# A small early read of w1's rows and a last tile cut 384 + 128, in a fused retention and MLP kernel

## The chip, the cores and the metric

The kernel runs on one core of a Trainium2 chip. The metric is device time in microseconds for one execution of the whole program. A core has five engines that run their own instruction streams in order: TensorE (PE, matrix multiplication), VectorE (DVE), ScalarE (ACT), GpSimd (POOL) and SyncE (SP, which here only issues transfers). Transfers between device memory and the core's own memory are issued from the queues of SP, ACT and POOL and carried out by 16 DMA engines.

## The reference

Two parts, one after the other. The first is a retention layer over 4 batches, 8 heads, 768 positions and a head size of 64; the second is a layer norm with a two-matrix MLP and a residual:

```python
for t in range(S):
    state = gamma * state + einsum('bhd,bhe->bhde', k[:, :, t], v[:, :, t])
    y[:, :, t] = scale * einsum('bhd,bhde->bhe', q[:, :, t], state)
x  = y.transpose(0, 2, 1, 3).reshape(B, S, 512)
xn = (x - mean(x)) / sqrt(var(x) + 1e-6) * g_ln
out = x + maximum(xn @ w_ch1, 0) @ w_ch2
```

`gamma` has one fixed value for each head. `w_ch1` is 512 x 2048, `w_ch2` is 2048 x 512; all inputs and the output are float32.

## The kernel before

**Tiles.** The 3072 positions are cut into 24 tiles of 128. The first four tiles are the first chunks of the four batches; after them come the five further chunks of each batch in turn. The recurrence is computed chunk by chunk: inside a chunk as a masked product of q and k (`pa`, L477), then with v (`py`, L505), between chunks through a state (`pd`, L551, with v scaled by GpSimd in `vg`, L539) that VectorE decays (`state`, L565) and TensorE multiplies with q (L501). VectorE takes the mean and variance (L520, L521) and subtracts the mean and multiplies by `g_ln` (`xn`, L515); ScalarE keeps a bf16 copy of the row (`x_all`, L526).

**The MLP.** The matrix w1 is loaded in four quarters of 512 columns and w2 in four quarters of 512 rows; each is converted to bf16 on the way, and such loads come from GpSimd's queue (L382; q, k and v on L374). Tiles are grouped by 1, 2 or 4. For each group TensorE multiplies the transposed `xn` with blocks of w1 (`mm`, L626; the block `ho` of 128 columns belongs to quarter `ho // 4`), ScalarE or, for the first tiles, VectorE applies the maximum with zero (L639, L641), and TensorE multiplies with w2 (`tp`, L664). VectorE scales by the reciprocal deviation and adds the residual (L673), and the result is stored (L680): from SP's queue, or from ACT's for a piece that doesn't begin at column 0. The last tile is done in two pieces of 256 columns, each with its 16 matmuls, its VectorE operation and its store.

**Transposes.** For the first eight tiles q, k (L437, L444) and `xn` (L579) are transposed by TensorE; from tile 8 on by DMA transposes from SP's queue (L459, L593).

**The order of the work.** Nothing is placed by hand. The kernel describes tasks with `plan.add` (engine, a cost in ns, a rank, what they come after, which buffer they take), and `Plan.order` plays a small model of the engines forward and emits each engine's instructions in the order that it finds: of all tasks that can start, the one with the earliest start, and at equal starts the one with the lower rank. Two numbers stand for the DMA engines: `sw_free`, when the queue of GpSimd's loads is believed to be empty, and `hw_free` for transfers of SP and ACT. A load pushes `sw_free` on by its cost (875 or 1250 ns for a tile of q, k or v, 2550 for a quarter of a weight) and is believed to be usable some time after. A transfer with a cost `hw` that finds loads queued pushes them too:

```python
            if t["hw"]:
                begun = max(at + 600, hw_free)
                queued = max(0, sw_free - begun)
                hw_free = begun + t["hw"] + min(queued, 2 * t["hw"])
                if queued:
                    sw_free += t["hw"] * 2 // 3
```

A load is not planned to be issued earlier than 7000 ns ahead of `sw_free`. The early loads follow the order of the list `first`, with v of tile 0 the first of them. `Plan.fill` puts dummy matmuls (L691) into holes of TensorE's plan up to 14 us. SP's early tasks are two loads of halves of k and q of tile 0 (L345) and the load of `g_ln` into `grow` (L312), in this order of rank; the first two have no `hw` cost in the plan and neither has `grow`. SP's next task after these is the first DMA transpose.

Of the kernel before, what the change touches and what calls it, by code (L numbers as in the profile page):

```python
# [9 lines left out]
FP32 = mybir.dt.float32  # L10
# [4 lines left out]
PE, ACT, DVE, POOL, SP = range(5)  # L15

CFG = {
    "T0": 8, "TX": 8, "groups": [1] * 8 + [2] * 4 + [4] * 2,
    "first": ["iota", "pos", "v0", "k1", "q1", "v1", "w1_0", "k2", "q2", "w1_1", "v2",
              "k3", "q3", "v3", "w1_2", "k4", "q4", "v4", "k5", "q5", "v5", "w1_3", "w2_0",  # L20
              "k6", "q6", "v6", "k7", "q7", "v7", "w2_1", "w2_2", "w2_3"],
    "bufs": {"qsb": 6, "ksb": 5, "vsb": 9, "qk": 8, "tr": 6, "vg": 3, "trq": 3, "trk": 3},
    "load_pad": 600, "w_pad": 1500, "lead": 32, "lead2": 32, "sq_at": 28000, "late_load": 1250, "step": 8, "pace": 8, "ahead": 3,
    "slack": 600, "tr_pad": 4000, "x_pad": 3000, "vg_pad": 1000, "fill": 0.8, "fill_end": 14000,
}

# [101 lines left out]
def kernel(  # L128
# [16 lines left out]
    nc = tc.nc  # L145

    B, H, S, D = q.shape
    DM = H * D
    DH = 4 * DM
    P = 128  # L150
    C = S // P
    NT = B * C
    KO = DM // P
# [31 lines left out]
    const = ctx.enter_context(tc.tile_pool(name="const", bufs=1))  # L185
# [12 lines left out]
    def take(pool, key, shape, dtype):  # L198
        held[pool, key] = pools[pool].tile(shape, dtype, name=pool, tag=pool)
        return held[pool, key]  # L200
# [5 lines left out]
    w1_v = moe_w_ch1.rearrange("(ko p) n -> p ko n", p=P)  # L206
# [21 lines left out]
    gb = const.tile([P, DM], FP32, name="gb")  # L228
    bns = const.tile([P, NT, 6], FP32, name="bns")
    mv = const.tile([P, NT, 2], FP32, name="mv")  # L230
    rstd = const.tile([P, NT], FP32, name="rstd")
    w1 = const.tile([P, KO, DH], BF16, name="w1")
    w2 = const.tile([P, HO, DM], BF16, name="w2")
# [55 lines left out]
    a = plan.add  # L289
# [18 lines left out]
    def c_gb(eng):  # L308
# [4 lines left out]
        out=grow, in_=moe_g_ln.rearrange("(o n) -> o n", o=1)), lat=2500)  # L313
# [85 lines left out]
        load(x, j, pool_rank.get(f"{x}_{j}" if x[0] == "w" else f"{x}{j}", 20 * i))  # L399
    for t, x in ((iota, "iota"), (ipos, "pos")):  # L400
        t["rank"] = pool_rank[x]

    unit, u, behind = {}, 0, []
    for g in range(NG):
# [12 lines left out]
    for t in range(NT):  # L417
        g, i = group_of[t]
# [6 lines left out]
    for t in range(NT):  # L425
# [31 lines left out]
        else:  # L457
            def e_tr(eng, t=t):
# [4 lines left out]
                   hw=1600, lat=TR_PAD)  # L463
# [67 lines left out]
        if c > 0:  # L531
            for cc in ([0, 1] if c == 1 else [c]):
                if cc == C - 1:
                    continue
                j = number[b, cc]
# [113 lines left out]

    loaded_w2 = [loaded["w2", i] for i in range(4)]  # L650
    for t, cols in [(t, slice(0, DM)) for t in range(NT - 1)] + [
            (NT - 1, slice(i * DM // 2, (i + 1) * DM // 2)) for i in range(2)]:
        g, i4 = group_of[t]
        hb, h0 = buf_of[g]
        key = ("tp", ("2", t, cols.start))
        w = cols.stop - cols.start
        dep = [relu[g, ho] for ho in range(0, HO, GMAX // GROUPS[g])]
        prev = None
        for part in range(4):
            def e_m2(eng, hb=hb, i=h0 + i4, key=key, part=part, cols=cols, w=w):  # L660
                if part == 0:
                    take(*key, [P, w], FP32)
                for ho in range(4 * part, 4 * part + 4):
                    nc.tensor.matmul(held[key], lhsT=held["h1", hb][:, ho, i * P:(i + 1) * P],  # L664
                                     rhs=w2[:, ho, cols], start=(ho == 0), stop=(ho == HO - 1))
            prev = a(PE, 865 * w // DM, 500 + unit["2", t] + part + (4 if cols.start else 0), e_m2,
                     dep[part * len(dep) // 4:(part + 1) * len(dep) // 4] + (loaded_w2 if part == 0 else [])
                     + ([prev] if prev else []),
                     key if part == 0 else None,
                     [("h1", hb)] + ([key] if part else []))  # L670

        def e_add(eng, t=t, key=key, cols=cols, w=w):
            nc.vector.scalar_tensor_tensor(  # L673
                out=take("osb", key, [P, w], FP32), in0=held[key], scalar=rstd[:, t:t + 1],
                in1=x_all[:, t, cols], op0=ALU.mult, op1=ALU.add)
        add = a(DVE, 750 * w // DM, -10, e_add, [prev, held["rs", t]], ("osb", key), [key])

        def e_st(eng, t=t, key=key, cols=cols):
            b, c = TILES[t]
            (nc.scalar if eng == ACT else nc.sync).dma_start(out=out_v[b, c, :, cols],  # L680
                                                             in_=held["osb", key])
        a(ACT if cols.start else SP, 400, 100, e_st, [add], uses=[("osb", key)], hw=450)
# [44 lines left out]
```

## Time and profile before

| | |
|---|---|
| median of 6 runs | 217.69 us (217.35 to 220.28) |
| profiled execution | 217.04 us |
| its span, first to last instruction | 215.0 us |
| mean granted TensorE clock | 0.998 |
| TensorE busy | 205.3 us (96%) |
| VectorE, ScalarE, GpSimd busy | 119.6, 83.8, 96.8 us |
| first use of w1 by TensorE | 13.0 us |
| last of GpSimd's quarters of weights issued | 34.3 us |

Times in the profile are microseconds from the start of the span unless marked ns. A line of a timeline gives the start, the length, the engine, the line of the program, the operation, `output<-input`, shapes and count, and in brackets the idle time before it and what ended that. "POOLq", "SPq" and "ACTq" are the queues' issuing instructions. The chain of waits follows the last instruction back to what released it, and so on to the start. A matmul's length is modelled, and runs of matmuls overlap by a fraction, so a busy TensorE isn't TensorE at its peak.

### The profile page before, as it was taken

What the parts mean: (1) busy time and instruction counts of PE and PEld (TensorE: products, weight loads), DVE (VectorE), ACT (ScalarE), POOL (GpSimd) and SP (SyncE); (2) the same over time, 40 slices, a digit from 0 to 9 for tenths busy, and PEclk for the clock granted to TensorE, in tenths of its full rate; (3) what the DMA queues carried; (4) which work ended last, traced back from release to release, by engine and by line L of the source; (5) the groups of instructions that cost most, each with busy time, mean ns of one, the idle gap of its engine ahead of it and who ended that gap; (6) DMA issues with size and microseconds to landing.
All of it is one profiled execution on the core that took longest, in us unless ns stands there. A gap on an engine that the chain in (4) does not pass through costs nothing.

```text
span 215.0 us, 4747 instructions
## 1 busy us (share of the span) xinstructions
PE 205.3 (96%) x1942; PEld 133.3 (62%) x1962; DVE 119.6 (56%) x230; ACT 83.8 (39%) x157; POOL 96.8 (45%) x151
## 2 busy tenths in 40 slices
PE   7968989999999999999999999999999999999993
PEld 3447979998755468677577667655454444444452
DVE  6767586992167775657997637866553411011121
ACT  5356675765420117245135324305554214442000
POOL 8998858735877745848776757000000000000000
PEclk9999999999999999999999999999999999999999
DMA  9999999999999999999999999921202121010212
GB/s 134 163 180 181 166 194 170 208 114 143 119 178 175 176 191 144 153 138 179 141 165 169 142 210 184 152 73 27 73 0 73 37 88 39 10 49 3 98 49 98
DMA packets 108359, 26.78 MB, mean 125 GB/s; under 512 B 101041, under 2 KB 105393, under 8 KB 108338
## 3 DMA queue, kind: packets, MB, share of 16 engines
q0 software_dynamic: 77024, 13.37, 84.8%
q1 hardware_dynamic: 30114, 12.72, 27.6%
q10 hardware_dynamic: 1200, 0.39, 0.7%
q8 instruction: 15, 0.25, 0.5%
q14 instruction: 6, 0.05, 0.1%
HBM read 27.27 MB, written 6.29 MB: 156 GB/s over the span
## 4 chain that ended last, share of the span: by engine, by line
PE 83%; POOL 10%; DMA 5%; issue 1%; DVE 0%; POOLq 0%
PE tp L664 38%; PE mm L626 35%; DMA w<-in_moe_w_ch_dram 5%; PE pa L477 3%; PE pd L551 2%; PE py L505 2%; POOL qsb L374 2%; PE py L501 2%; POOL v L374 2%; POOL w L382 1%; POOL k L374 1%; POOL vg L539 1%; POOL vsb L374 1%; POOL ksb L374 1%; POOL state L287 0%
## 5 line engine op out<-in xcount | busy, mean ns | idle before, releaser
L626 PE MATMUL mm<-xnt,w 128*128 128x128 bf16 (+2 forms) x896 | 93.4, 257 | 1.0 <-ACT xnt L203 1.0
L664 PE MATMUL tp<-w,h 128*128 128x512 bf16 (+1 forms) x381 | 86.9, 370 | 1.1 <-issue 0.2
L639 ACT ACTIVATE h<-mm 128x512 bf16<-128x512 f32 x91 | 54.4, 598 | 66.2 <-PE mm L626 65.8
L626 PEld LDWEIGHTS <-w 128*128 128x128 bf16 x896 | 66.2, 98 | 21.2 <-issue 1.0
L664 PEld LDWEIGHTS <-h 128*128 128x128 bf16 x400 | 37.7, 98 | 37.5
L673 DVE SCALAR_TENSOR_TENSOR osb<-tp,rstd,x_all 128x512 f32<-128x512 f32 (+1 forms) x25 | 18.2, 728 | 51.6 <-PE tp L664 51.5
L488 DVE TENSOR_TENSOR asb<-pa,mask 128x1024 bf16<-128x1024 f32 x24 | 29.3, 1221 | 12.9 <-PE pa L477 12.8
L520 DVE BATCH_NORM_STATS2 bns<-py 128x6 f32<-128x512 f32 x24 | 16.7, 694 | 17.0 <-PE py L505 17.0
L526 ACT CAST x_all<-py 128x512 bf16<-128x512 f32 x24 | 14.0, 584 | 28.6 <-DVE xn L515 28.0
L539 POOL TENSOR_TENSOR vg<-vsb,vsc 128x512 bf16<-128x512 bf16 x16 | 16.6, 1042 | 12.6 <-PE mm L626 5.5
L374 POOL DMA_DIRECT2D vsb<-in_v_dram x20 | 18.2, 909 | 0.8 <-issue 0.4
L515 DVE SCALAR_TENSOR_TENSOR xn<-py,mv,gb 128x512 bf16<-128x512 f32 x24 | 18.0, 751 | 0.9
L565 DVE TENSOR_TENSOR state<-pd,gch 64x256 bf16<-64x256 f32 x40 | 16.7, 418 | 2.5 <-PE pd L551 2.2
L374 POOL DMA_DIRECT2D qk<-in_q_dram x16 | 14.0, 877 | 2.7 <-issue 1.9
L374 POOL DMA_DIRECT2D qk<-in_k_dram x16 | 14.1, 883 | 1.4 <-issue 0.8
L387 POOL COPY scrap<-qk 1x1 bf16<-1x1 bf16 x30 | 5.3, 177 | 12.8 <-DMA qk<-in_q_dram 6.4
L466 DVE TENSOR_TENSOR trq<-tr,qsc 128x512 bf16<-128x512 bf16 x16 | 8.5, 530 | 2.9 <-DMA tr<-qk 2.8
L691 PE MATMUL pd<-zeros 128*128 128x512 bf16 (+1 forms) x23 | 7.0, 442 | 1.2 <-DVE zeros L237 1.2
L601 ACT ACTIVATE rstd<-mv,epsb 128x1 f32<-128x1 f32 (+2 forms) x14 | 3.8, 289 | 11.2 <-DVE mv L521 11.2
L505 PE MATMUL py<-vsb,asb 128*128 128x64 bf16 x160 | 7.9, 193 | 0.0
L501 PEld LDWEIGHTS <-trq 128*128 128x128 bf16 x80 | 6.0, 98 | 3.1
L505 PEld LDWEIGHTS <-asb 128*128 128x128 bf16 x192 | 7.9, 98 | 0.0
(64 smaller groups left out, 122.1 us busy)
## 6 DMA issues: line engine op xcount, KB each, us to landing
out_dram<-osb SPq DMA_DIRECT2D x23, 256.0 KB, 2.2
w<-in_moe_w_ch_dram POOLq DMA_DIRECT2D x8, 512.0 KB, 9.7
vsb<-in_v_dram POOLq DMA_DIRECT2D x20, 128.0 KB, 5.2
qk<-in_k_dram POOLq DMA_DIRECT2D x16, 128.0 KB, 4.8
qk<-in_q_dram POOLq DMA_DIRECT2D x16, 128.0 KB, 5.1
qsb<-in_q_dram POOLq DMA_DIRECT2D x7, 128.0 KB, 8.0
v<-in_v_dram POOLq DMA_DIRECT2D x4, 128.0 KB, 6.5
ksb<-in_k_dram POOLq DMA_DIRECT2D x4, 128.0 KB, 9.1
```

What stands on the lines that cost most here:

```text
L374: nc.gpsimd.dma_start(out=tile_of(kind, j), in_=src)
L488: nc.vector.tensor_tensor(out=take("asb", t, [P, NPAIR, 2, P], BF16).rearrange("p i a t -> p a i t"), in0=held["pa", t], in1=mask.rearrang ...
L505: nc.tensor.matmul(py[:, h, :], lhsT=held["asb", t][:, h // 2, h % 2, :], rhs=tile_of("v", t)[:, h, :], start=(mi == 0), stop=(mi == n - 1))
L515: nc.vector.scalar_tensor_tensor(out=take("xn", t, [P, DM], BF16), in0=held["py", t].rearrange("p h d -> p (h d)"), scalar=mv[:, t, 0:1], ...
L520: nc.vector.bn_stats(out=bns[:, t, :], in_=held["py", t].rearrange("p h d -> p (h d)"))
L526: nc.scalar.copy(out=x_all[:, t, :].rearrange("p (h d) -> p h d", d=D), in_=held["py", t])
L539: e.tensor_tensor(out=take("vg", j, [P, H, D], BF16), in0=tile_of("v", j), in1=vsc[:, cc, :].unsqueeze(2).to_broadcast([P, H, D]), op=ALU. ...
L565: nc.vector.tensor_tensor(out=held["pb", n][o, :, o], in0=held["pd", b][o, :, o], in1=gch[o, cc, :].unsqueeze(2).to_broadcast([D, NPAIR, D ...
L626: nc.tensor.matmul(p[:, j, :], lhsT=w1[:, ko, (ho + j) * P:(ho + j + 1) * P], rhs=held["xnt", hb][:, h0:h0 + n, ko, :], start=(ko == 0), s ...
L639: nc.scalar.activation(out=dst, in_=src, func=AF.Relu)
L664: nc.tensor.matmul(held[key], lhsT=held["h1", hb][:, ho, i * P:(i + 1) * P], rhs=w2[:, ho, cols], start=(ho == 0), stop=(ho == HO - 1))
L673: nc.vector.scalar_tensor_tensor(out=take("osb", key, [P, w], FP32), in0=held[key], scalar=rstd[:, t:t + 1], in1=x_all[:, t, cols], op0=AL ...
```

## The change

There are two edits.

A new transfer is planned on SP with rank -140, behind `grow` (rank -150). It reads the first 16 columns of all 512 rows of w1, 64 bytes from each row, as float32 into a new tile `touch` that nothing reads. It carries `hw=400` in the plan.

The last tile's pieces come from a list in the configuration: columns 0 to 384 and 384 to 512, where they were 0 to 256 and 256 to 512. The code of a piece is the same; the first is stored from SP's queue and the second from ACT's.

```diff
-    "load_pad": 600, "w_pad": 1500, "lead": 32, "lead2": 32, "sq_at": 28000, "late_load": 1250, "step": 8, "pace": 8, "ahead": 3,
+    "load_pad": 600, "w_pad": 1500, "lead": 32, "lead2": 32, "sq_at": 28000, "late_load": 1250, "tail": (0, 384, 512), "step": 8, "pace": 8, "ahead": 3,
...
+    touch = const.tile([P, KO, 16], FP32, name="touch")
...
+    a(SP, 390, -140, lambda eng: nc.sync.dma_start(out=touch, in_=w1_v[:, :, 0:16]), hw=400)
+
     unit, u, behind = {}, 0, []
...
     for t, cols in [(t, slice(0, DM)) for t in range(NT - 1)] + [
-            (NT - 1, slice(i * DM // 2, (i + 1) * DM // 2)) for i in range(2)]:
+            (NT - 1, slice(i, j)) for i, j in zip(CFG["tail"], CFG["tail"][1:])]:
```

## The prediction

> **What bounds the kernel now.** I read the granted clock first (0.998, so nothing of the clock is in play), then the busy times by stretch, then the chain that ended last, then the order of instructions around the chain's turning point, and last the final microseconds.
>
> ```profile
> core 0: us, PE busy (x) PEld busy (x) DVE busy (x) ACT busy (x) POOL busy (x), PEclk, DMA share, GB/s
> 0.00:10.00 10.00, 8.76 (x60) 4.32 (x62) 6.77 (x32) 5.19 (x13) 9.22 (x16) 1.00 1.34 147
> 10.00:20.00 10.00, 7.87 (x122) 6.26 (x120) 7.30 (x13) 5.20 (x10) 9.87 (x13) 1.00 1.85 180
> 20.00:34.00 14.00, 12.12 (x222) 11.46 (x223) 9.73 (x21) 8.93 (x19) 10.03 (x12) 1.00 1.92 177
> 34.00:50.00 16.00, 15.95 (x290) 15.11 (x289) 13.88 (x28) 11.47 (x23) 9.86 (x14) 1.00 1.50 163
> 50.00:150.00 100.00, 99.21 (x927) 66.34 (x938) 64.85 (x112) 34.07 (x62) 57.87 (x98) 1.00 1.52 151
> ```
>
> These are stretches of the span with each engine's busy time. Past 34 us TensorE is idle 0.05 us in 16 and 0.79 us in 100: that part is TensorE's own work and has almost nothing to give. All that can be won lies ahead of 34 us (5.2 us idle, part of the rest dummy matmuls) and after the last matmul.
>
> ```profile
> 19.11 0.88 POOL vsb L374
> 20.20 9.89 DMA w<-in_moe_w_ch_dram
> 30.09 0.62 issue
> 30.72 0.75 POOL w L382
> 31.48 1.06 POOL vg L539
> ...
> 32.59 0.38 PE pd L551 x4
> 32.97 1.79 PE mm L626 x32
> ```
>
> This is the chain of waits, in order of time. Up to 20 us it is GpSimd issuing loads back to back; then the landing of the fourth quarter of w1 (issued at 20.20) releases GpSimd's issue of a quarter of w2, `vg` of tile 4 stands behind that issue, and TensorE's state update `pd` behind `vg`. From 32.59 on TensorE never waits long again, so **whatever stands ahead of `pd` in TensorE's order is free, and what stands behind it costs its full length.**
>
> ```profile
> 30.35 1.07 PE L626 MATMUL mm<-xnt,w 128*128 128x128 bf16 x16
> ...
> 32.59 0.38 PE L551 MATMUL pd<-vg,ksb 128*128 128x128 bf16 x4 [1.17 <-POOL vg L539]
> ```
>
> The timeline shows 1.17 us of idle TensorE at that point. Finally the end:
>
> ```profile
> 211.72 0.48 DVE L673 SCALAR_TENSOR_TENSOR osb<-tp,rstd,x_all 128x256 f32<-128x256 f32 x1 [1.21 <-PE tp L664]
> 212.23 0.37 ACTq L680 DMA_DIRECT2D out_dram<-osb  x1
> ```
>
> The last matmul is followed by 0.48 us of VectorE, an issue from ScalarE's queue, and a store which lands 1.7 us after its issue, at 213.93; about 1.07 us of closing work fill the span of 215.0.
>
> **What the Trainium skill says.** "DMA: Bandwidth & Descriptors", section "Issuing engines are not separate DMA queues": transfers started from different engines run on the same 16 DMA engines and interleave. So the small transfer from SyncE isn't free beside GpSimd's loads; the trace agrees that these are backed up (a load issued at 3.32 us takes 4.5 us to land, one issued at 10.0 us takes 8.4). The same page, "Measured": about 10.5 ns for a packet. The trace gives 13 ns: loads of 1024 pieces of 256 B land 0.83 us apart while the queue is full, 64 pieces per engine. The same page, "Specifications": rows under 512 B are not moved at line rate; the small transfer's pieces are 64 B and the last store's rows become exactly 512 B. No operation of the kernel before moves 64 B pieces.
>
> **The tail.** The last tile is 512 columns, now cut 384 and 128. TensorE does 16 matmuls of 384 and 16 of 128 columns in place of 32 of 256. Before, 32 take 3.45 us, 108 ns each; 384 columns scale to 162 ns, and the trace has 128-column matmuls at 56 ns (0.89 us for 16). So 2.59 + 0.89 = 3.48, a change of +0.03. VectorE's last operation: 0.75 us for 512 columns and 0.48 for 256 put 128 columns at about 0.35, which saves 0.13. The store: 256 KB land in 2.2 us (median), 128 KB in 1.7; 64 KB lie between 1.45 (the slope carried on) and 1.7, which saves 0 to 0.25. The first piece must not become the last: its matmuls end at 209.98 + 0.86 = 210.84, VectorE takes 0.61, SyncE issues at 211.5, and 192 KB land in about 1.95, at 213.45, ahead of the last piece's 213.55 to 213.8. Taken: **-0.2**, from 0 to -0.35.
>
> **The small transfer's own cost.** 128 partitions by 4 row blocks are 512 pieces of 64 B, 32 for each DMA engine. It is issued on SyncE behind the 0.40 us issue of `grow`, at about 2.2 us; SyncE's next task is at 47.13, so its queue holds nobody up, and nobody reads what it brings. What it costs is time of the DMA engines, ahead of all loads from then on: 32 x 13 ns = 0.42 us at the packed rate. The upper bound is the mean time of a packet on GpSimd's queue: 84.8% of 16 x 215 us over 77024 packets is 38 ns, 1.2 us in all. The lower bound is a gain: the first quarter of w1 lands 11.64 - 8.67 = 2.97 us after the load ahead of it, the second 15.93 - 13.4 = 2.5; if the excess of 0.47 is a first visit to those rows, the transfer could take it away and itself hide in the first 5 us, when the engines' share was 0.90 against 1.8 later. The backlog never empties before 30 us, so a delay reaches the fourth quarter's landing, and by the chain above the end, in full. Taken: **+0.4**, from -0.5 to +1.2.
>
> **What it moves: the planner's order.** `Plan.order` gives each engine its order ahead of time. The new task has `hw=400`; with its turn at 2,090 ns it finds software loads queued, and line 99 adds 400 x 2 // 3 = 266 ns to `sw_free`. Only v of tile 0 was taken before that, so every later load is believed to land 266 ns later. I followed the start times by hand. At about 12.1 us the matmuls of tile 1 (`py`, due 12,290) now start ahead of k of tile 2 (due 12,125, now 12,391); the trace has TensorE waiting for that k until 12.56, so `py` comes nearly a microsecond earlier, but this doesn't move the gate at 32.59. At the gate it does matter: `vg` of tile 4 was due at 31,020, 100 ns before TensorE was free for `pd`; it is now due at 31,286. TensorE's believed times there are not pushed by loads (no hole in the plan from 21,530 on) and come out somewhat earlier, near 30,890. So the next block of 16 matmuls, the first on the fourth quarter of w1 (due 30,566), is put **ahead** of `pd`. That block takes 0.89 us and now fills the idle 1.17: **-0.89**, the rest of the stall stays. VectorE's chain behind `pd` starts as before and finds the next relu sooner (it waited 0.86 us for it at 34.80), so I expect the gain to hold. Bounds: 0 if I slipped in following the plan, -1.2 if the whole stall goes. The extra dummy matmuls that the planner may put into a longer hole (two of 58 ns) lie in idle time.
>
> **Sum.** -0.89 + 0.4 - 0.2 = -0.69. The profiled execution took 217.04 us for its span of 215.0, so 216.35; it stands 0.65 below the median of the runs, 217.69, on which the forecast is 217.0.
>
> **Rivals.**
> A, as above: 217.0, chance 0.50.
> B, the order near `pd` stays; the transfer delays the gate by 0.4 to 1.2 and the tail gives 0.2: 217.9 to 218.7, say 218.2, chance 0.15. For it: the margin at the choice is a hundred to a few hundred ns, found by hand.
> C, the early read does what its place suggests and spares the first quarter's 0.47 at no cost of its own: -0.89 - 0.47 - 0.2 = -1.56, 216.1, up to -2.3 if further early waits go; chance 0.13. Against it: the first quarter of w2 is also new to the DMA engines and shows no excess (32.6 after 30.1).
> D, slower. The plan's choices change behind the gate too. VectorE is busy 13.88 of the 16 us from 34 to 50; relus of the first six tiles may go to ScalarE or VectorE, whichever the planner finds free sooner. Three more at 0.69 us fit in VectorE's 2.12 us of idle time; from the fourth on each delays the chain from mask to normalisation which TensorE waits for. With eight, 8 x 0.69 - 2.12 = 3.4, and -0.69 + 3.4 gives 220.4; chance 0.22. For it: TensorE has no idle time past 34 us to lose, only to gain. Against: the same 266 ns make the planner more careful of loads everywhere.
>
> **How the numbers follow.** About 1% is what a measurement of this kernel can tell from no change; that is 2.2 us. Faster by more needs the far end of C and part of A: 0.16. Slower by more is most of D and little of B: 0.21. The rest, 0.63, lies within. The range leaves out the far ends of C and D: 215.4 to 219.9.
>
> **What would show it.** Right: a block `mm` between 31.4 and `pd`, with the wait for `vg` at some 0.3 us; `py` of tile 1 ahead of k of tile 2 near 11.7; the fourth quarter of w1 landing within 0.5 us of 30.1; the last VectorE operation at 0.35 us. Wrong: new TensorE idle time between 34 and 150 us above the 0.84 now, more VectorE relus (B would show the old order and a later landing), or a first quarter that lands early.

## The result, and the profile after

The changed kernel takes 216.51 us (median of 31 runs, 214.98 to 218.10) beside 217.74 us for the kernel before (66 runs). The ratio is 0.9938, with a 95% interval of 0.9923 to 0.9953: 1.35 us less, between 1.0 and 1.7. The forecast was 0.69 us less, at 217.0. The sign is as forecast; the gain is twice as large. The range on record, 215.4 to 219.9, holds the result, but it would have held no change and a slowdown too.

The profiled execution took 216.59 us, with a span of 214.8. That is only 0.2 us under the span of before, because the profiled execution of before was one of its quick ones (217.04 beside a median of 217.74). So the profiles show where instructions stand, and the sizes have to come from the repeated runs.

First the busy times by stretch, with the columns as before:

```profile
core 0: us, PE busy (x) PEld busy (x) DVE busy (x) ACT busy (x) POOL busy (x), PEclk, DMA share, GB/s
0.00:10.00 10.00, 8.47 (x60) 3.97 (x62) 6.55 (x32) 5.08 (x13) 9.23 (x16) 1.00 1.36 148
10.00:20.00 10.00, 7.64 (x121) 6.26 (x120) 6.73 (x11) 5.01 (x9) 9.06 (x13) 1.00 1.85 180
20.00:34.00 14.00, 13.14 (x240) 12.30 (x238) 10.27 (x22) 10.30 (x20) 10.62 (x14) 1.00 1.91 177
34.00:50.00 16.00, 16.00 (x296) 15.43 (x295) 14.02 (x29) 11.08 (x23) 8.97 (x12) 1.00 1.48 156
50.00:150.00 100.00, 98.45 (x906) 64.84 (x918) 67.36 (x115) 33.96 (x62) 59.73 (x101) 1.00 1.53 152
```

Between 20 and 34 us TensorE now works 13.14 us instead of 12.12. Some of this is given back: from 50 to 150 us it is idle 1.55 us, where it was 0.79. New idle time in this part is one of the signs that the prediction named for its being wrong.

Then the chain of waits and TensorE's timeline around the state update of tile 4:

```profile
5.12 7.41 DMA w<-in_moe_w_ch_dram
12.53 0.28 issue
12.81 0.76 POOL w L383
...
30.97 1.89 PE mm L629 x32
32.89 0.38 PE pd L554 x4
33.27 0.89 PE mm L629 x16
```

```profile
11.82 0.41 PE L508 MATMUL py<-v,asb 128*128 128x64 bf16 x8
13.45 0.40 PE L440 MATMUL tp<-idn,k 128*128 128x128 bf16 x4 [1.23 <-DMA k<-in_k_dram]
...
30.90 1.96 PE L629 MATMUL mm<-xnt,w 128*128 128x128 bf16 x32
32.89 0.38 PE L554 MATMUL pd<-vg,ksb 128*128 128x128 bf16 x4
```

Both exchanges that were worked out by hand are there: `py` of tile 1 stands ahead of k of tile 2, and 32 matmuls instead of 16 stand ahead of the state update, which no longer waits. GpSimd's `vg` is no part of the chain at this point any more: the chain now goes back along TensorE's work, and at its start GpSimd's issue at 12.81, to the landing of w1's first quarter at 12.53, where the chain of before turned at the landing of the fourth. GpSimd's two `vg` take 2.06 us from 31.78, so the first ends near 32.8; without the block of 0.89 us ahead of it, TensorE would have stood at the state update at 32.0. TensorE starts on the k of tile 2 at 13.45, against 12.56 before.

Last the end, from the timeline:

```profile
211.00 0.62 DVE L676 SCALAR_TENSOR_TENSOR osb<-tp,rstd,x_all 128x384 f32<-128x384 f32 x1 [1.91 <-PE tp L667]
211.84 0.35 DVE L676 SCALAR_TENSOR_TENSOR osb<-tp,rstd,x_all 128x128 f32<-128x128 f32 x1 [0.22 <-PE tp L667]
212.22 0.36 ACTq L683 DMA_DIRECT2D out_dram<-osb  x1
```

The last VectorE operation takes 0.35 us, and its store lands 1.6 us after its issue, at 213.85; the store of the first piece has landed before, at 213.46. From the last VectorE operation's start to that landing it is 2.0 us, where it was 2.2.

### The profile page after: what moved, and what is told of

It is laid out like the page before. It is cut to its first block, busy times and chain, and to the rows that moved or that the text cites. A ratio compares the mean times of both kernels' runs of the same rounds, so it can differ in the third digit from the quotient of the medians.

```text
span 214.8 us, 4757 instructions
## 1 busy us (share of the span) xinstructions
PE 205.2 (96%) x1944; PEld 132.1 (62%) x1964; DVE 120.6 (56%) x230; ACT 83.5 (39%) x157; POOL 97.6 (45%) x151
## 4 chain that ended last, share of the span: by engine, by line
PE 84%; DVE 5%; DMA 3%; POOL 3%; issue 2%; ACT 1%; POOLq 0%
PE mm L629 38%; PE tp L667 34%; DMA w<-in_moe_w_ch_dram 3%; PE pa L480 3%; PE pd L554 2%; PE py L508 2%; PE py L504 2%; DVE trq L469 2%; POOL v L375 1%; DVE bns L523 1%; DVE osb L676 1%; DVE state L568 1%; PE tp L582 1%; PE tp L440 1%; DVE asb L491 1%
## 5 line engine op out<-in xcount | busy, mean ns | idle before, releaser
L667 PE MATMUL tp<-w,h 128*128 128x512 bf16 (+2 forms) x381 | 87.2, 370 | 1.3 <-issue 0.5
L667 PEld LDWEIGHTS <-h 128*128 128x128 bf16 x400 | 37.0, 98 | 38.3
L676 DVE SCALAR_TENSOR_TENSOR osb<-tp,rstd,x_all 128x512 f32<-128x512 f32 (+2 forms) x25 | 18.2, 728 | 46.6 <-PE tp L667 46.4
L469 DVE TENSOR_TENSOR trq<-tr,qsc 128x512 bf16<-128x512 bf16 x16 | 10.4, 652 | 4.9 <-DMA tr<-qk 4.8
L383 POOL DMA_DIRECT2D w<-in_moe_w_ch_dram x8 | 6.2, 771 | 3.9 <-DMA w<-in_moe_w_ch_dram 3.9
```

Of the source, the lines that this page charges most:

```text
L469: nc.vector.tensor_tensor(out=take("trq", t, [P, NPAIR, P], BF16), in0=held["tr", t][:, 0:NPAIR, :], in1=qsc, op=ALU.mult)
L676: nc.vector.scalar_tensor_tensor(out=take("osb", key, [P, w], FP32), in0=held[key], scalar=rstd[:, t:t + 1], in1=x_all[:, t, cols], op0=AL ...
```

## The experiments

Two theories stood at first. **Order**: the planner's new order gains, the transfer costs, the tail gives 0.2 us. **The read pays**: the early visit to w1's rows gains by itself. A third, **tail**, is settled on the way. All ratios are to the kernel before on the same chip. None of the kernels leaves out computation.

### The tail alone

```diff
-    a(SP, 390, -140, lambda eng: nc.sync.dma_start(out=touch, in_=w1_v[:, :, 0:16]), hw=400)
```

(taken from the changed kernel; the tail of 384 and 128 stays, and so does the tile `touch`)

> The kernel before with the last tile cut 384 + 128 and nothing else. Theory 'order' (most of the gain is the planner's new order, the tail gives 0.2 us): -0.2 us, a ratio of 0.999; the last VectorE operation 0.35 us, the last store landing 0.1 to 0.3 us sooner after the last matmul. Rival 'tail' (the shorter end carries the gain): -1.0 us or more, a ratio of 0.995.

Measured: 0.9995 (0.9973 to 1.0016), 217.57 us. Nothing that can be told from 0, and the forecast 0.2 us lies inside the interval. The tail doesn't carry the gain.

### The order alone

```diff
-    a(SP, 390, -140, lambda eng: nc.sync.dma_start(out=touch, in_=w1_v[:, :, 0:16]), hw=400)
+    a(SP, 390, -140, lambda eng: None, hw=400)
```

(and the tail back at 256)

> The planner is told of the small transfer (its task with hw=400 stays in the plan) but nothing is issued, and the tail is 256 + 256: only the order of the instructions differs from the kernel before. Theory 'order': -0.9 to -1.3 us, a ratio of 0.994 to 0.996, the state update of tile 4 at about 32.6 us with a wait of 0.3 us or less, a block of 16 matmuls ahead of it. Rival 'the read pays' (the early read of the rows is what gains): 0, a ratio of 1.000.

Measured: 0.9962 (0.9942 to 0.9982), -0.83 us, 216.99 us. The planner's 266 ns gain without any transfer, a little less than this theory expected. The block stands ahead of the state update, which doesn't wait:

```profile
31.09 1.96 PE L629 MATMUL mm<-xnt,w 128*128 128x128 bf16 x32
33.08 0.38 PE L554 MATMUL pd<-vg,ksb 128*128 128x128 bf16 x4
```

GpSimd's first `vg` ends at 33.03 here. Without the block TensorE would have arrived at 32.19 and waited 0.84 us.

Two things go beyond the two exchanges. The order differs in many more places: side by side, the traces of before and of this run disagree on TensorE, VectorE, ScalarE and SyncE again and again until past 130 us. And the time of an execution less its span, the part that no profile line covers, is 1.77 us in the mean here and 1.77 to 1.79 in all five kernels with the new order, but 1.92 to 1.99 in every kernel with the old one (1.96 before). So some 0.18 of the 0.83 us stand outside the span. What causes that is open.

### The transfer alone

```diff
-    a(SP, 390, -140, lambda eng: nc.sync.dma_start(out=touch, in_=w1_v[:, :, 0:16]), hw=400)
+    a(SP, 390, -140, lambda eng: nc.sync.dma_start(out=touch, in_=w1_v[:, :, 0:16]))
```

(and the tail back at 256)

> The small transfer is issued but the planner isn't told (no hw cost), so every engine's order is that of the kernel before; the tail is 256 + 256. Theory 'order': the transfer only costs, +0.3 to +0.8 us, a ratio of 1.001 to 1.004; the first loads land some 0.8 us later and the state update of tile 4 starts at 32.9 us. Rival 'the read pays': -0.5 us or more, a ratio of 0.998 or less.

Measured: 0.9972 (0.9960 to 0.9984), **-0.61 us**, 217.29 us. This falls against the theory that was on record: the transfer gains, with every engine's order unchanged (the traces agree, `touch` apart). All of it lies within the span. The three parts multiply to 0.9995 x 0.9962 x 0.9972 = 0.9929, within the interval of the whole change.

### One exchange alone, in the kernel before

```diff
...
-        for t in plan.fill(plan.order(), PE, 1100, FILL_END, FILL, warm):
+        tasks = plan.order()
+        gate, block = (next(t for t in tasks if t.get("name") == x) for x in ("pd4", "mm0_12"))
+        tasks.remove(block)
+        tasks.insert(tasks.index(gate), block)
+        for t in plan.fill(tasks, PE, 1100, FILL_END, FILL, warm):
```

(the two tasks are given the names `pd4` and `mm0_12`)

> The kernel before with one exchange in TensorE's order: the first block of 16 matmuls on the fourth quarter of w1 goes ahead of the state update of tile 4. No transfer, no other change. Theory 'order', narrow form (this one exchange is the gain): -0.6 to -0.9 us, a ratio of 0.996 to 0.997, and the wait at the state update falls from 1.2 to 0.3 us. Rival 'the order elsewhere' (the gain comes from other places of the new order, or is given back by VectorE behind the gate): within 0.2 us of no change.

Measured: 0.9993 (0.9972 to 1.0015), 217.66 us. Nothing that can be told from 0; the interval is -0.6 to +0.3 us. The number is what the rival 'the order elsewhere' expected. Its timeline says why this can be:

```profile
13.96 0.40 PE L437 MATMUL tp<-idn,k 128*128 128x128 bf16 x4 [2.02 <-DMA k<-in_k_dram]
...
32.34 1.96 PE L628 MATMUL mm<-xnt,w 128*128 128x128 bf16 x32
34.14 0.39 PE L551 MATMUL pd<-vg,ksb 128*128 128x128 bf16 x4
```

In this execution the k of tile 2 came 1.4 us later than in the profile of before, with no transfer to delay it, and TensorE's granted clock was at half from 15.3 to 18.7 us. TensorE then reaches the state update at 34.14 and waits for nothing; without the exchange it would have arrived 0.89 earlier, at 33.25, just as `vg` ends (two of them take 2.05 us from 32.29, so the first ends at about 33.3). In this execution the exchange has almost nothing to fill. So the 1.17 us in the profile of before need not be typical.

This gave a new theory, **late TensorE**: two paths meet at the state update, GpSimd's (landing of w1's fourth quarter, issue, `vg`) and TensorE's own work counted from the landing of k of tile 2; the exchange counts only where TensorE is in time. Four runs followed, and then four more.

### The same transfer from w2's rows

```diff
-    a(SP, 390, -140, lambda eng: nc.sync.dma_start(out=touch, in_=w1_v[:, :, 0:16]))
+    a(SP, 390, -140, lambda eng: nc.sync.dma_start(out=touch, in_=w2_v[:, 0:KO, 0:16]))
```

> As the run with the transfer alone, but its 512 pieces of 64 bytes come from the first 512 rows of w2, not from w1; same place, same size, orders of the kernel before. Theory 'first visit' (the first quarter of w1 lands late because nobody has read those rows yet, and the early read takes this over): no gain, 0 to +0.5 us, and the first quarter of w1 still lands 3.0 us or more after the v load ahead of it. Rival 'any early transfer' (the transfer gains by its timing or by what it pushes, wherever it reads): -0.6 us again, and 2.5 us between the two landings.

Measured: 0.9979 (0.9956 to 1.0001), 217.17 us. The time is near that of the transfer from w1, though its interval just reaches no change; the landing of w1's first quarter, 13.1 us with 4.2 after the v ahead of it, is what "first visit" said. Half of each expectation holds.

### `py` of tile 1 first, in the kernel before

The same edit as for the exchange above, with the task `py1` put ahead of the transposes of k of tile 2.

> The kernel before with one other exchange in TensorE's order: the py matmuls of tile 1 ahead of the transposes of k of tile 2 (some dummy matmuls more stand in the hole before). Theory 'late TensorE' (in most runs TensorE reaches the state update of tile 4 late and waits for nothing there, so that what counts is work counted from the landing of that k): -0.2 to -0.5 us, a ratio of 0.998 to 0.999. Rival 'gate' (the prediction's: only what stands ahead of the state update counts): 0, a ratio of 1.000.

Measured: 1.0007 (0.9989 to 1.0026), 217.77 us. No gain (the interval is -0.2 to +0.6 us), so "late TensorE" missed here: even where TensorE is late, 0.24 us of work done ahead of that landing doesn't show in the time. The prediction had given this exchange no worth of its own.

### The exchange undone in the changed kernel

The code of the exchange above, in the changed kernel, with the block put behind the state update.

> The changed kernel with the one exchange undone: the state update of tile 4 again ahead of the first block on the fourth quarter of w1. Theory 'late TensorE': with the transfer the k of tile 2 lands sooner, TensorE is in time, so that here the exchange counts: 0.3 to 0.9 us of the gain is lost, a ratio of 0.996 to 0.998, and a wait of 0.5 us or more at the state update. Rival 'the exchange is worth nothing, as in the run with it alone': the ratio stays at 0.994.

Measured: 0.9972 (0.9956 to 0.9988), 217.14 us, against 0.9938 with it. **The exchange is worth 0.0034, or 0.74 us**, in the changed kernel (0.3 to 1.2 by an estimate from the two intervals), and the wait is back:

```profile
31.34 1.07 PE L631 MATMUL mm<-xnt,w 128*128 128x128 bf16 x16
33.29 0.38 PE L554 MATMUL pd<-vg,ksb 128*128 128x128 bf16 x4 [0.88 <-POOL vg L542]
33.51 1.95 PE L631 MATMUL mm<-xnt,w 128*128 128x128 bf16 x32
```

### A sparse early read

```diff
-    a(SP, 390, -140, lambda eng: nc.sync.dma_start(out=touch, in_=w1_v[:, :, 0:16]), hw=400)
+    a(SP, 390, -140, lambda eng: nc.sync.dma_start(
+        out=touch[0:P // 8], in_=moe_w_ch1.rearrange("(ko p s) n -> s p ko n", p=P // 8, s=8)[0, :, :, 0:16]), hw=400)
```

> The changed kernel with an early read of every eighth row of w1, 64 pieces of 64 bytes in place of 512; all else the same. Theory 'first visit' with a reach of more than one row: the first quarter of w1 still lands 2.5 us after the v load ahead of it, and the first loads of v and k land sooner, so -0.1 to -0.5 us against the changed kernel, a ratio of 0.991 to 0.993. If each row has to be visited by itself: the landing gap goes back to 3.0 us or more and the ratio to 0.996.

Measured: 0.9951 (0.9931 to 0.9971), 216.67 us. It can't be told from the changed kernel's 0.9938, nor from the 0.9957 that order and tail give together. In its profile the first quarter of w1 lands 3.8 us after the v ahead of it. The gap is what the second expectation named, the ratio lies between the two.

### GpSimd's gate taken away, in the kernel before

```diff
...
+        tasks = plan.order()
+        first, then = next(t for t in tasks if t.get("name") == "vg4"), loaded["w2", 1]
+        tasks.remove(first)
+        tasks.insert(tasks.index(then), first)
...
```

> The kernel before with one exchange in GpSimd's order: vg of tile 4 ahead of the issue of w2's second quarter, so that it no longer stands behind the landing of w1's fourth quarter. Theory 'gate' (the prediction's): the wait at the state update of tile 4 goes, -0.7 to -1.2 us, a ratio of 0.995 to 0.997. Theory 'late TensorE' (in typical runs of the kernel before TensorE gets there late by itself): 0 to -0.4 us, a ratio of 0.998 to 1.000.

Measured: 0.9974 (0.9953 to 0.9994), -0.57 us, 217.15 us. It lies between what the two theories gave: the gate is worth something in the kernel before. The interval, 0.1 to 1.0 us, doesn't decide whether that is less than the 0.89 of the prediction. In its profile the state update, at 33.44, waits for nothing.

### The same transfer from rows that the kernel reads anyway, ahead of it

```diff
-    a(SP, 390, -140, lambda eng: nc.sync.dma_start(out=touch, in_=w1_v[:, :, 0:16]))
+    a(SP, 390, -140, lambda eng: nc.sync.dma_start(
+        out=touch, in_=k[0].rearrange("h (c p) d -> c p h d", p=P)[0][:, 0:KO, 0:16]))
```

> As the run with the transfer alone, but its 512 pieces of 64 bytes come from k of tile 0, which has been read already. Theory 'first visit of w1': no gain, 0 to +0.5 us. Rival 'any early transfer' (with whatever it reads): -0.4 to -0.6 us, a ratio of 0.997 to 0.998, and a low share of runs with a clock below 0.996 (it was 5% with either transfer, 25% without).

Measured: 0.9974 (0.9958 to 0.9990), -0.57 us, 217.34 us. It reads nothing of w1 and gains as much. (The rows of k had been asked for before it, at 0.7 us, but landed only at 3.4 to 3.7, after its issue at 2.2.) "First visit of w1" falls as the explanation of the transfer's gain. The other half of that expectation missed: 6 of its 22 runs had a clock under 0.996, as without a transfer.

### Two transfers

One more `dma_start` of the same form, of columns 16 to 32, into a second tile.

> As the run with the transfer alone, with a second one of the same size behind it that reads columns 16 to 32 of the same rows. Theory 'first visit of w1': the rows have been visited, the second only costs engine time: +0.2 to +0.5 us against one transfer, a ratio of 0.998 to 1.000. Rival 'any early transfer': the gain stays or grows, 0.997 or less.

Measured: 0.9979 (0.9960 to 0.9999), 217.16 us. Neither more gain than one transfer nor a cost that shows; the number lies on the edge between the two expectations and decides nothing.

### GpSimd's gate taken away in the changed kernel

The edit that put `vg4` ahead of the second quarter of w2, now in the changed kernel.

> The changed kernel with vg of tile 4 ahead of the issue of w2's second quarter in GpSimd's order: a candidate that could beat both kernels. Theory 'gate': in the changed kernel the block of matmuls already covers most of the wait, so 0 to -0.4 us against it, a ratio to the kernel before of 0.992 to 0.994. Rival 'late issue' (the quarter of w2 issued a microsecond later costs more than the wait saved): a ratio of 0.995 or more.

Measured: **0.9917 (0.9893 to 0.9941), 215.85 us**. This is the lowest ratio of the study, 1.8 us under the kernel before; its interval overlaps with that of the changed kernel, so that it beats it is likely and not shown. "Late issue" falls. GpSimd's timeline:

```profile
28.30 0.91 POOL L375 DMA_DIRECT2D vsb<-in_v_dram  x1
29.19 1.09 POOL L542 TENSOR_TENSOR vg<-vsb,vsc 128x512 bf16<-128x512 bf16 x1
30.86 0.82 POOL L383 DMA_DIRECT2D w<-in_moe_w_ch_dram  x1 [0.58 <-DMA w<-in_moe_w_ch_dram]
```

`vg` now runs in the time in which GpSimd would wait for the landing, and the quarter of w2 is issued no later (30.86, against 31.01 in the changed kernel).

## Why the prediction was right, and where it was not

**The order, -0.89.** Right in mechanism and place, and in size within the intervals. The state update lost its wait, the block stands where it was worked out to stand, and undoing this one exchange in the changed kernel costs 0.74. The order alone gives -0.83 (0.4 to 1.3), but it differs at other places too, and 0.18 of its gain lies outside the span. What the prediction didn't see is that the exchange depends on TensorE being in time. It took the 1.17 us of the profile of before for the rule. Set side by side, the profiles of kernels with the order of before near the state update show how far the early landings spread:

| profile | k of tile 2 used | wait for it | state update | wait there |
|---|---|---|---|---|
| before | 12.56 | 0.95 | 32.59 | 1.17 |
| transfer alone | 12.95 | 1.00 | 33.32 | 1.29 |
| tail alone | 13.05 | none | 32.68 | 0.30 |
| two transfers | 13.19 | 1.24 | 32.56 | 0.52 |
| transfer, k rows | 13.87 | 1.66 | 33.35 | none |
| transfer, w2 rows | 13.97 | 1.77 | 33.39 | 0.56 |
| `py` first | 14.22 | 2.26 | 35.11 | none |

With k at 13.2 us or sooner the wait is 0.3 to 1.3 us, with k near 14 it is 0 to 0.6. The seven waits are 0.55 us in the mean, close to the 0.57 that taking the gate away gained. A block of 0.89 would fill 0.45 of them; that is an estimate, and the interval of the exchange alone in the kernel before, -0.6 to +0.3, can't exclude it. So the 0.83 of the whole order and the two exchanges alone (no gain shown) don't contradict each other for certain: the intervals of the whole order and of the first exchange overlap. How much of the 0.83 belongs to the other places of the new order is not settled; the two exchanges were not run together without them.

**The transfer, +0.4.** This is the step that failed: "a delay reaches the fourth quarter's landing, and by the chain above the end, in full." Alone the transfer gains 0.61 (0.35 to 0.87). The cost at the start is there, and larger than taken: on SyncE's queue the packets' share of the first 36 us rises from 3.2% to 5.1%, which is 0.7 us of each DMA engine or 21 ns for a piece, not 13; and with 512 pieces the first v lands at 6.0 to 6.5 us in seven profiles, without a transfer at 5.5 to 6.0 in six. But the delay doesn't reach the fourth quarter's landing in any way that shows: that lies between 30.1 and 30.9 us in the eight profiles with a transfer and between 30.1 and 32.1 in the six without. Executions differ by more than the delay, and the end comes sooner. The lower bound, a gain of 0.5, had the right size and, as the explanation of the gain, the wrong reason: rows of w2 and rows of k gain 0.46 and 0.57. That the result lies in the range in spite of this term is owed to the width of the range. What such a transfer does for the time is **open**; no run moved it to another time or queue.

One thing was seen with it: the runs with a TensorE clock under 0.996 are 45 of 205 for the kernel before and 1 of 22 each for the transfer alone from w1, from w2 and twice, and 1 of 31 for the changed kernel. But the k rows gain too, with 6 of 22; without any transfer the order alone has 2 of 18 and `py` first 2 of 22; and among the runs with a full clock the transfer from w1 is still ahead of the kernel before (medians 217.28 and 217.70). In the kernel before, the runs with the lower clock are 0.1 to 0.6 us longer in the median, so a share that falls from 45 of 205 to 1 of 22 is worth about 0.1 us at most by this estimate. The clock is at most a small part.

**The tail, -0.2.** The operation took 0.35 us as worked out, and the end from VectorE's last start to the landing is 0.2 us shorter in the profile. The repeated runs, -0.1 with an interval of about 0.5 to either side, can't confirm it.

**The sum.** -0.89 + 0.4 - 0.2 = -0.69 on record; with the measured parts -0.83 - 0.61 - 0.1 = -1.54, and -1.35 for the whole. The term that was wrong is the transfer: +0.4 on record, -0.61 measured.

**The rivals.** B (the order near the state update stays) is refuted by the profile. C (the early read pays at no cost of its own) gave -1.56, close to the result, and its mechanism, the first visit to w1, isn't what gains: the k rows gain as much. Something of it may be in the landings: the gap from the v load to w1's first quarter is 2.5 to 3.4 us in the five profiles that read all of w1's rows early and 3.0 to 4.5 in the other nine. D (new idle time behind the gate) is there in small: 0.76 us more idle time from 50 to 150 us, in the one profile, and not by its relus: VectorE does 5 of the 96 in both kernels.

## What to carry to other kernels

A wait in one profiled execution is a sample: where two paths meet within a microsecond, look at several executions before pricing the removal of either. A transfer that nobody waits for can act through a planner's bookkeeping as well as through the DMA engines, so run both halves apart. And where an engine waits for a landing with ready work queued behind that wait, try the work first: `vg` ahead of the issue gained 0.57 us in the kernel before.

## What the runs showed of the hardware that was not expected

In all 14 profiles GpSimd never issues a load before the load eight places ahead of it in its queue has landed; the closest is 0.28 us after that landing. This is where the gate comes from: the second quarter of w2 (issued at 30.72 before) is the eighth load after the fourth quarter of w1 (landed at 30.09), and the third quarter of w1 is the eighth after the first (12.81 and 12.53 in the changed kernel). Whether the limit is the chip's or the framework's, no run shows.

The landing of the first quarter of w1, issued at 5.0 to 5.2 us in every kernel, lies between 11.7 and 13.3 us in profiles without a transfer (11.7, 12.2, 12.7, 13.1, 13.3 and 13.3), and between 12.1 and 13.1 with one. The k of tile 2 lands 0.8 to 0.9 us after it in each; the fourth quarter follows only in part.

When TensorE waits long for k of tile 2, its granted clock can fall to a half for 3 to 7 us afterwards. The windows of the run with the one exchange (wait of 2.02 us, ended at 13.96) show it in the third column from the right:

```profile
13.00:15.00 2.00, 1.04 (x23) 1.04 (x24) 0.37 (x1) 0.58 (x1) 1.64 (x3) 1.00 1.42 200
15.00:17.00 2.00, 1.78 (x21) 1.53 (x18) 1.71 (x5) 1.18 (x2) 2.00 (x4) 0.58 2.08 165
17.00:19.00 2.00, 1.87 (x24) 1.60 (x23) 1.95 (x3) 0.58 (x1) 2.00 (x3) 0.57 2.22 170
19.00:21.00 2.00, 2.00 (x44) 2.00 (x42) 0.53 (x1) 1.36 (x3) 1.91 (x3) 1.00 1.44 196
```

The same was seen with waits of 2.26 and 2.81 us, and once with 1.66; not with 1.77, 1.51, 1.41 or less. In the profile of the tail alone it fell to a half from 8.1 to 11.5 us, with no such wait. It may explain part of TensorE's late arrivals at the state update in the table above; no run was made to show it.
